# Attention and feed-forward on one core: the second batch's q and k turned on TensorE, the first batch reordered

## The chip, the cores and the metric

The kernel runs on one core of a Trainium2 chip. The metric is the device time of one execution in microseconds, shown as the median of the runs.

## The reference

For 8 batches the reference computes grouped-query attention, with 16 query heads over 4 key/value heads, 384 tokens and head width 64, and then a feed-forward layer whose activation is a squared ReLU:

```python
k, v = repeat(k, 4), repeat(v, 4)                   # 4 -> 16 heads
attn = softmax(q @ k.T / 8)                         # per head, 384 x 384
x    = (attn @ v) -> [3072 tokens, 1024]
h    = max(x @ w_in, 0)                             # 1024 -> 2048
out  = (h * h) @ w_out                              # 2048 -> 1024
```

Inputs and output are float32; the kernel multiplies in bfloat16.

## The kernel before, in words

The work is cut into 64 pairs of heads, eight to a batch (`NPB`); pair p belongs to batch p // 8. A pair needs kT (the keys of its key/value head, turned so that the head width lies on the partitions, and doubled, so that both heads of a pair have a copy) and qT (its queries, turned alike). TensorE forms the scores of a pair into PSUM, ScalarE takes their exponential (`expT`), TensorE multiplies it with the values, which carry a column of ones, into `po` (`attend`, L382), and VectorE divides by the column sums (L389, L392) into `o_sb`. The result is turned once more into `xT`, the feed-forward's input. A batch's feed-forward has 128 up matmuls (16 tiles of 8, L408) and 96 down matmuls (6 tiles of 16, L426). Each up tile is clipped on VectorE and squared on ScalarE into `h2T`; each down tile is copied to `y_sb` and stored from SP's queue.

A `Recorder` (L8) takes every operation in program order, with the tiles that it reads and writes, and adds the semaphore waits. Each engine issues its own operations strictly in recorded order, so whatever is recorded behind a waiting operation on the same engine waits too.

**First batch.** Its q, k and v come by plain loads; GpSimd casts q chunk by chunk (`cast_q`, L228) and between the casts issues the loads of `w_in` in eight parts. kT, qT and xT are turned on TensorE by `turn_on_pe` (L268): three 128x128 transposing matmuls against an identity into a PSUM bank, and a VectorE copy out (L278). Scores come in three units a pair (`scores_unit`, L332, two matmuls at L339), each with its own exponential (L345) and two sets of PSUM banks in turn. Matmuls on a zeroed tile (`idle`, L252) fill the gaps.

**Later batches.** `prepare(b)` (L298) doubles k on VectorE (L301), then issues three DMA transposes from SP's queue: kT (L304), and qT in two halves (L311, pairs 0 to 3 and 4 to 7 of the batch), and then the loads of k and q for batch b + 2 from GpSimd's queue. `prepare_v` does the values. For batch 1, `prepare(1)` is called inside the first feed-forward; for the others, in the fifth pair of the batch before (`n % NPB == 4`). Scores of a pair come in one go (`scores_pair`, L348, matmuls at L355) with one exponential (L372). `put_x` (L395) turns `o_sb` into `xT` by a DMA transpose on SP's queue.

**Order.** `feed_forward` is a generator of steps of four matmuls. `fill(ns)` records as many steps as a budget buys, at 165 ns an up matmul and 216 ns a down matmul; `ready` holds the last batch whose feed-forward may run. After the first batch, `fill(8000)`, `prepare(1)`, `prepare_v(1)` and `fill(12000)` come before pair 8. Then each pair records its scores, a fill of 0.4, the values of the head before, a fill of 0.2, the other head, `put_x`, and a fill of 0.4 of `PER_PAIR`, which is 2600 in batch 1 (pairs 8 to 15) and 5000 after it. While pairs 8 to 15 run, only the first feed-forward may be drawn from, so it has to last for them; the second one may begin with pair 17.

Of the kernel before, what the change touches and what calls it, by code (L numbers as in the profile page):

```python
# [5 lines left out]
ALU = mybir.AluOpType  # L6
# [100 lines left out]
def bass_gqa_attention__then__ffn_squared_relu_kernel(  # L107
# [12 lines left out]
    HKV = 4  # L120
# [37 lines left out]
    po = nc.alloc_psum_tensor("po", [128, 512], f32)  # L158
    f_ps = [nc.alloc_psum_tensor(f"f_ps{i}", [128, 512], f32) for i in range(2)]
    po_v = po[:, 0:NJ * 2 * (D + 1)].rearrange("p (i s e) -> p i s e", i=NJ, s=2)  # L160
    sc_flat = sc_ps.ap().rearrange("p b c -> p (b c)")


# [64 lines left out]
    def cast_q(c):  # L228
        R.add("gpsimd", lambda g: g.tensor_copy(q_st[0][:, 2 * c:2 * c + 2, :], q_f[:, 2 * c:2 * c + 2, :]),  # L229
              reads=[("q_f", c)], writes=[("q_st", 0, c)])  # L230

    cast_q(0)
    cast_q(1)
    R.add("gpsimd", lambda g: g.tensor_copy(
        v_aug[0][:, :, 0:D], v_f.ap().rearrange("p g j d -> p (g j) d")),
        reads=["v_f"], writes=[("v_aug", 0)])
    load_w_in(0)
    for c in range(2, NPB):
        cast_q(c)
        load_w_in(c - 1)  # L240
# [11 lines left out]
    def idle(count):  # L252
# [4 lines left out]

        R.add("tensor", mm, reads=["warm"], writes=[("f_ps", 1)])


    banks = [0]

    def turn_bank():
        i = banks[0] % 2
        banks[0] += 1
        return [(sc_ps[:, 4].bitcast(bf16), ("sc", 4)), (f_ps[0].ap().bitcast(bf16), ("f_ps", 0))][i]

    def turn_on_pe(src, src_keys, dst, dst_key):  # L268
        ps, key = turn_bank()

        def tr(pe):
            for t in range(NJ):
                m = pe.matmul(ps[:, t * 128:(t + 1) * 128], src[:, t * 128:(t + 1) * 128], ident[:],  # L273
                              is_transpose=True)
            return m

        R.add("tensor", tr, reads=[*src_keys, "ident"], writes=[key])
        R.add("vector", lambda e: e.tensor_copy(dst, ps[:, 0:S]), reads=[key], writes=[dst_key])  # L278

    def dup_k(b, g):  # L280
        src = (k_f if b == 0 else k_st[b % NKS])[:, g].unsqueeze(2).to_broadcast([128, NJ, 2, D])
        R.add("vector", lambda e: e.tensor_copy(k_dup[b % 2][:, g * NJ:(g + 1) * NJ], src),
              reads=[("k_f", g) if b == 0 else ("k_st", b % NKS)], writes=[("k_dup", b % 2, g)])

    def first_kT(g):
        dup_k(0, g)
        turn_on_pe(k_dup[0][:, g * NJ:(g + 1) * NJ].rearrange("p a x d -> p (a x d)"), [("k_dup", 0, g)],
                   kT[0][:, g], ("kT", 0, g))

    def first_qT(c):  # L290
        turn_on_pe(q_st[0][:, 2 * c:2 * c + 2, :].rearrange("p h e -> p (h e)"), [("q_st", 0, c)],
                   qT[0][:, c], ("qT", 0, c))

    def first_oT(c):
        turn_on_pe(o_sb[c % NO].ap().rearrange("p i s d -> p (i s d)"), [("o_sb", c % NO)],
                   xT[0][:, c], ("xT", 0, c))

    def prepare(b):  # L298
        st = b % NST
        src = k_st[b % NKS].ap().rearrange("p g j d -> p (g j) d").unsqueeze(2)  # L300
        R.add("vector", lambda e: e.tensor_copy(  # L301
            k_dup[b % 2][:, :, :, :], src.to_broadcast([128, HKV * NJ, 2, D])),
            reads=[("k_st", b % NKS)], writes=[("k_dup", b % 2, g) for g in range(HKV)])
        R.add("sync", lambda e: e.dma_start_transpose(  # L304
            kT[b % 2].ap().rearrange("p g (j c) -> p (g j) c", j=NJ),
            k_dup[b % 2].ap().rearrange("p a x d -> p (a x d)")),
            reads=[("k_dup", b % 2, g) for g in range(HKV)],
            writes=[("kT", b % 2, g) for g in range(HKV)], dma=f"kt{b % 2}")
        for part in range(2):
            cs = range(4 * part, 4 * part + 4)  # L310
            R.add("sync", lambda e, cs=cs: e.dma_start_transpose(  # L311
                qT[b % 2][:, cs.start:cs.stop, :].rearrange("p h (t c) -> p (h t) c", t=NJ),
                q_st[st][:, 2 * cs.start:2 * cs.stop, :].rearrange("p h e -> p (h e)")),
                reads=[("q_st", st, c) for c in cs], writes=[("qT", b % 2, c) for c in cs],
                dma=f"qt{b % 2}_{part}")
        if b + 2 < B and b >= 1:
            load_k(b + 2)
            if b > 1:
                load_q(b + 2)

    def prepare_v(b):
        R.add("vector", lambda e: e.tensor_copy(
# [49 lines left out]
        R.add("scalar", lambda e: e.activation(dst, src, AF.Exp, scale=0.125),  # L372
              reads=sc_keys, writes=[("expT", p % NEX, j) for j in range(NJ)])

    def attend(p, s):
        b, g = p // NPB, (p % NPB) // 2

        def av(pe):
            for i in range(NJ):
                f = NJ * s + i  # L380
                for j in range(NJ):
                    m = pe.matmul(po_v[:, i, s, :], expT[p % NEX][:, j, f * 128:(f + 1) * 128],  # L382
                                  v_aug[b % 2][:, g * NJ + j, :], start=(j == 0), stop=(j == NJ - 1))
            return m

        R.add("tensor", av, reads=[("expT", p % NEX, j) for j in range(NJ)] +
              [("v_aug", b % 2), ("v_one", b % 2)], writes=["po"])
        if s == 1:
            R.add("vector", lambda e: e.reciprocal(rinv[p % 2].ap().unsqueeze(3), po_v[:, :, :, D:D + 1]),  # L389
                  reads=["po"], writes=[("rinv", p % 2)])  # L390
            rb = rinv[p % 2].ap().unsqueeze(3).to_broadcast([128, NJ, 2, D])
            R.add("vector", lambda e: e.tensor_tensor(o_sb[p % NO][:, :, :, :], po_v[:, :, :, 0:D], rb, ALU.mult),  # L392
                  reads=["po", ("rinv", p % 2)], writes=[("o_sb", p % NO)])

    def put_x(p):  # L395
        b, c = p // NPB, p % NPB
        R.add("sync", lambda e: e.dma_start_transpose(
            xT[b % NXT][:, c, :].rearrange("p (i c) -> p i c", i=NJ),
            o_sb[p % NO].ap().rearrange("p i s d -> p (i s d)")),
            reads=[("o_sb", p % NO)], writes=[("xT", b % NXT, c)], dma=f"xt{p % 8}")  # L400


    tiles = [0]

    def up_step(b, c, half, u, r):
        def mm(pe):
            for kc in range(4 * half, 4 * half + 4):
                m = pe.matmul(f_ps[u][:, 0:S], w_in_sb[:, kc, c * 128:(c + 1) * 128],  # L408
                              xT[b % NXT][:, kc, :], start=(kc == 0), stop=(kc == NKC - 1))
            return m  # L410

        R.add("tensor", mm, reads=[("w_in", c * 128 // WC)] +
              [("xT", b % NXT, kc) for kc in range(4 * half, 4 * half + 4)], writes=[("f_ps", u)])
        if half == 1:
            R.add("vector", lambda e: e.tensor_scalar_max(hr[r][:, :], f_ps[u][:, 0:S], 0.0),  # L415
                  reads=[("f_ps", u)], writes=[("hr", r)])
            R.add("scalar", lambda e: e.activation(h2T[b % 2][:, c, :], hr[r][:, :], AF.Square),  # L417
                  reads=[("hr", r)], writes=[("h2T", b % 2, c)])
        return 4 * 165

    def down_step(b, i, jj, part, u):
        yb = (b * 2 * NJ + jj * NJ + i) % NY
# [17 lines left out]
        return 4 * 216  # L440

    def feed_forward(b):
        for c in range(NFC):
            for half in range(2):
                yield up_step(b, c, half, tiles[0] % 2, tiles[0] % NHR)
            tiles[0] += 1
        for jj in range(2):
            for i in range(NJ):
                for part in range(4):
                    yield down_step(b, i, jj, part, tiles[0] % 2)  # L450
                tiles[0] += 1


    ready = [-1]

    def all_feed_forward():
        for b in range(B):
# [3 lines left out]

    ffn = all_feed_forward()
    credit = [0.0]
    FIRST, SECOND = 8000.0, 12000.0
    PER_PAIR = {1: 2600.0, **{b: 5000.0 for b in range(2, B + 1)}}

    def fill(ns):
        credit[0] += ns
# [4 lines left out]
                return  # L473
            credit[0] -= t

    idle(12)
    first_kT(0)
    first_qT(0)
    first_qT(1)
    for n in range(NPB):  # L480
        scores_unit(n, 0)
        if n + 2 < NPB:
            if n % 2 == 0:
                first_kT((n + 2) // 2)
            first_qT(n + 2)
        else:
            idle(1)
        scores_unit(n, 1)
        idle(1)
        if n >= 1:  # L490
            attend(n - 1, 0)
        scores_unit(n, 2)
        idle(1)
        if n >= 1:
            attend(n - 1, 1)
        if n >= 2:
            first_oT(n - 2)
    idle(2)
    attend(NPB - 1, 0)
    first_oT(NPB - 2)  # L500
    attend(NPB - 1, 1)
    idle(5)
    first_oT(NPB - 1)
    load_q(3)
    ready[0] = 0
    fill(FIRST)
    prepare(1)
    prepare_v(1)
    fill(SECOND)
    for n in range(NPB, NP + 1):  # L510
        per = PER_PAIR[n // NPB]
        if n < NP:
            scores_pair(n)
        fill(per * 0.4)
        if n > NPB:
            attend(n - 1, 0)
        fill(per * 0.2)
        if n > NPB:
            attend(n - 1, 1)
            put_x(n - 1)  # L520
        if n % NPB == 4 and n // NPB + 1 < B:
            prepare(n // NPB + 1)
        if n % NPB == 7 and n // NPB + 1 < B:
            prepare_v(n // NPB + 1)
        fill(per * 0.4)
        ready[0] = max(0, n // NPB - 1)
# [32 lines left out]
```

## Time and profile before

| | us |
|---|---|
| median of 3 runs (464.14 to 468.75) | 466.71 |
| the profiled execution | 464.65 |
| its span, first to last instruction | 462.9 |

The span is what the trace's times count from; some 1.75 us of the profiled execution lie around it. PE is TensorE's matmul row, DVE is VectorE, ACT is ScalarE, POOL is GpSimd, SP the engine whose queue carries stores and DMA transposes. A busy share is an average over stages; which wait ends last in a stage is read from the chain of waits and from the timeline.

### The profile page before, as it was taken

Reading aid. Unit: us, or ns where it says so; the run is one execution under the profiler, and the core shown is the slowest. Engines: PE = TensorE matmul, PEld = TensorE weight load, DVE = VectorE, ACT = ScalarE, POOL = GpSimd, SP = SyncE. Lnnn points to the kernel's source line nnn. Section 1 sums busy time; section 2 is a strip of 40 time slices with the busy share of each in tenths; the row PEclk is TensorE's granted clock in tenths of the full one; section 3 lists DMA queues with packets and bytes.
Section 4 is the critical chain, followed back from the end, with each engine's and each line's share of the span. In section 5 each row is a group of like instructions: output and inputs, shape, how many; then the busy total and the mean of one; then the engine's idle time right before and its main releaser. Section 6 shows DMA issues by size and latency. Waiting matters only on the chain.

```text
span 462.9 us, 8137 instructions
## 1 busy us (share of the span) xinstructions
PE 433.8 (94%) x3557; PEld 241.0 (52%) x3593; DVE 162.9 (35%) x343; ACT 199.2 (43%) x209; POOL 33.3 (7%) x48
## 2 busy tenths in 40 slices
PE   7889729968999999999999999999999999999997
PEld 3455415535654466555654566555654566545543
DVE  2454302323432344323443344223443244323411
ACT  3673315534663355434663266434562366302300
POOL 6921000200020001000020000000000000000000
PEclk9999959988999999999999999999999999999999
DMA  9999999592049411982099115221152210121012
GB/s 236 197 196 204 194 181 176 115 185 77 13 55 176 139 41 20 169 152 64 18 121 186 64 33 101 62 86 62 28 111 64 76 41 19 41 84 39 0 59 79
DMA packets 100643, 45.88 MB, mean 99 GB/s; under 512 B 79104, under 2 KB 94464, under 8 KB 100608
## 3 DMA queue, kind: packets, MB, share of 16 engines
q0 software_dynamic: 34288, 16.65, 28.6%
q1 hardware_dynamic: 64208, 27.15, 25.1%
q10 hardware_dynamic: 2112, 1.57, 1.1%
q8 instruction: 28, 0.46, 0.4%
q14 instruction: 7, 0.06, 0.0%
HBM read 35.65 MB, written 12.58 MB: 104 GB/s over the span
## 4 chain that ended last, share of the span: by engine, by line
PE 90%; DMA 5%; DVE 2%; issue 2%; POOL 1%; SPq 0%; ACTq 0%
PE f_ps L426 36%; PE f_ps L408 35%; PE po L382 8%; PE sc_ps L355 7%; DMA qT<-q_st 4%; PE sc_ps L339 1%; PE f_ps L255 1%; DMA q_f<-in_q_dram 1%; DVE o_sb L392 1%; DMA xT<-o_sb 1%; PE sc_ps L273 0%; PE f_ps L273 0%; DVE hr L415 0%; POOL q_st L229 0%; DVE xT L278 0%
## 5 line engine op out<-in xcount | busy, mean ns | idle before, releaser
L408 PE MATMUL f_ps<-xT,w_in_sb 128*128 128x384 bf16 x1024 | 181.2, 327 | 2.3 <-DMA xT<-o_sb 1.9
L426 PE MATMUL f_ps<-w_out_sb,h2T 128*128 128x512 bf16 x732 | 177.9, 382 | 2.3 <-issue 0.5
L372 ACT ACTIVATE expT<-sc_ps 128x2304 bf16<-128x2304 f32 x56 | 116.8, 2086 | 111.7 <-PE sc_ps L355 110.4
L408 PEld LDWEIGHTS f_ps<-xT,w_in_sb 128*128 128x128 bf16 x1024 | 94.5, 98 | 65.7 <-issue 6.8
L417 ACT ACTIVATE h2T<-hr 128x384 bf16<-128x384 f32 x128 | 66.7, 521 | 117.1 <-DVE hr L415 115.9
L415 DVE TENSOR_SCALAR hr<-f_ps 128x384 f32<-128x384 f32 x128 | 71.3, 557 | 116.8 <-PE f_ps L408 116.8
L426 PEld LDWEIGHTS f_ps<-w_out_sb,h2T 128*128 128x128 bf16 x768 | 69.0, 98 | 76.9 <-issue 8.4
L435 DVE COPY y_sb<-f_ps 128x512 f32<-128x512 f32 x48 | 33.2, 692 | 114.0 <-PE f_ps L426 113.5
L382 PEld LDWEIGHTS po<-v_aug,expT 128*128 128x128 bf16 x1152 | 54.5, 99 | 22.3 <-DVE o_sb L392 0.8
L382 PE MATMUL po<-v_aug,expT 128*128 128x65 bf16 x1152 | 58.5, 196 | 0.6 <-DVE o_sb L392 0.5
L355 PE MATMUL sc_ps<-qT,kT 64*128 64x128 bf16 (+2 forms) x504 | 38.6, 279 | 14.9 <-DMA qT<-q_st 11.0
L355 PEld LDWEIGHTS sc_ps<-qT,kT 64*128 64x128 bf16 x504 | 21.3, 96 | 36.6 <-issue 20.9
L392 DVE TENSOR_TENSOR o_sb<-po,rinv 128x384 bf16<-128x384 f32 x64 | 35.7, 557 | 2.2
L389 DVE RECIPROCAL rinv<-po 128x6 f32<-128x6 f32 x64 | 12.3, 192 | 54.1 <-PE po L382 54.1
L345 ACT ACTIVATE expT<-sc_ps 128x768 bf16<-128x768 f32 x24 | 18.4, 811 | 9.3 <-PE sc_ps L339 9.1
L166 POOL DMA_DIRECT2D k_st<-in_k_dram x7 | 5.3, 760 | 196.8 <-DVE k_dup L301 179.7
L255 PE MATMUL f_ps<-warm 128*128 128x256 bf16 x37 | 9.6, 343 | 1.1 <-DVE warm L220 1.1
L339 PE MATMUL sc_ps<-qT,kT 64*128 64x384 bf16 x48 | 9.6, 397 | 0.0
L180 POOL DMA_DIRECT2D q_st<-in_q_dram x7 | 8.2, 1173 | 1.5 <-PE sc_ps L339 1.5
L188 POOL DMA_DIRECT2D w_in_sb<-in_moe_w_in_dram x8 | 7.2, 896 | 0.0
L255 PEld LDWEIGHTS f_ps<-warm 128*128 128x128 bf16 x37 | 4.0, 113 | 5.7 <-issue 4.0
L173 POOL DMA_DIRECT2D v_st<-in_v_dram x7 | 5.5, 780 | 0.0
(34 smaller groups left out, 40.3 us busy)
## 6 DMA issues: line engine op xcount, KB each, us to landing
out_dram<-y_sb SPq DMA_DIRECT2D x48, 256.0 KB, 2.0
q_st<-in_q_dram POOLq DMA_DIRECT2D x7, 768.0 KB, 12.7
w_in_sb<-in_moe_w_in_dram POOLq DMA_DIRECT2D x8, 512.0 KB, 11.5
w_out_sb<-in_moe_w_out_dram POOLq DMA_DIRECT2D x2, 2048.0 KB, 36.0
k_st<-in_k_dram POOLq DMA_DIRECT2D x7, 192.0 KB, 4.1
v_st<-in_v_dram POOLq DMA_DIRECT2D x7, 192.0 KB, 14.2
xT<-o_sb SPq DMA_TRANSPOSE x56, 2.4
q_f<-in_q_dram ACTq DMA_DIRECT2D x1, 768.0 KB, 7.8
```

Of the source, the lines that this page charges most:

```text
L255: m = pe.matmul(f_ps[1][:, 0:256], warm[:, 0:128], warm[:, 0:256])
L339: m = pe.matmul(sc_ps[:, 2 * u + x, 0:S], kt[rows, j * 128:(j + 1) * 128], qt[rows, :])
L345: R.add("scalar", lambda e: e.activation(dst, src, AF.Exp, scale=0.125), reads=[("sc", 2 * u), ("sc", 2 * u + 1)], writes=[("expT", p % NE ...
L355: return pe.matmul(sc_flat[:, at + c0:at + c1], kt[rows, j * 128:(j + 1) * 128], qt[rows, c0:c1])
L372: R.add("scalar", lambda e: e.activation(dst, src, AF.Exp, scale=0.125), reads=sc_keys, writes=[("expT", p % NEX, j) for j in range(NJ)])
L382: m = pe.matmul(po_v[:, i, s, :], expT[p % NEX][:, j, f * 128:(f + 1) * 128], v_aug[b % 2][:, g * NJ + j, :], start=(j == 0), stop=(j == N ...
L392: R.add("vector", lambda e: e.tensor_tensor(o_sb[p % NO][:, :, :, :], po_v[:, :, :, 0:D], rb, ALU.mult), reads=["po", ("rinv", p % 2)], wr ...
L408: m = pe.matmul(f_ps[u][:, 0:S], w_in_sb[:, kc, c * 128:(c + 1) * 128], xT[b % NXT][:, kc, :], start=(kc == 0), stop=(kc == NKC - 1))
L415: R.add("vector", lambda e: e.tensor_scalar_max(hr[r][:, :], f_ps[u][:, 0:S], 0.0), reads=[("f_ps", u)], writes=[("hr", r)])
L417: R.add("scalar", lambda e: e.activation(h2T[b % 2][:, c, :], hr[r][:, :], AF.Square), reads=[("hr", r)], writes=[("h2T", b % 2, c)])
L426: m = pe.matmul(f_ps[u][:, :], h2T[b % 2][:, c, i * 128:(i + 1) * 128], w_out_sb[:, c, jj * 512:(jj + 1) * 512], start=(c == 0), stop=(c = ...
L435: R.add("vector", lambda e: e.tensor_copy(y_sb[yb][:, :], f_ps[u][:, :]), reads=[("f_ps", u)], writes=[("y", yb)])
```

## The change

On TensorE, kT and qT of batch 1 are turned by the first batch's functions, spread over the fills of the first feed-forward, into sc_ps banks 0 to 3; the three DMA transposes of batch 1 fall away. The fills before pair 8 become 6000, 1500, four of 700 and eight of 500; `PER_PAIR` of batch 1 becomes 3200. `prepare(2)` is called in pair 14 instead of pair 12; the later ones stay where they were. In the first batch, kT and qT are turned one pair ahead, behind the second score unit, most `idle` matmuls are placed anew, six two-chunk steps of the first two up tiles are recorded in pairs 5 and 6 and behind pair 7, and the last pair's two heads are normalised separately. The first load of `w_in` is issued ahead of the second cast of q. The diff, cut to its core:

```diff
 # setup
+    po_alt = sc_ps[:, 1, 0:NJ * 2 * (D + 1)].rearrange("p (i s e) -> p i s e", i=NJ, s=2)
...
     cast_q(0)
+    load_w_in(0)
     cast_q(1)
...                                            # (cast of v stands here)
-    load_w_in(0)
     for c in range(2, NPB):
...
+    def idle_on_sc(count):                      # idle() into sc_ps bank 3
...
-    banks = [0]
-    def turn_bank():
-        i = banks[0] % 2
-        banks[0] += 1
-        return [(sc_ps[:, 4].bitcast(bf16), ("sc", 4)), (f_ps[0].ap().bitcast(bf16), ("f_ps", 0))][i]
-    def turn_on_pe(src, src_keys, dst, dst_key):
-        ps, key = turn_bank()
+    slots = [0]
+    RING, FREE = (4, 5), (0, 1, 2, 3)           # 0 to 4: sc_ps banks; 5: f_ps[1]
+    def turn_bank(banks):
+        i = banks[slots[0] % len(banks)]
+        slots[0] += 1
+        if i == 5:
+            return f_ps[1].ap().bitcast(bf16)[:, 0:S], ("f_ps", 1)
+        return sc_bf[:, i, 0:S], ("sc", i)
+    def turn_on_pe(src, src_keys, dst, dst_key, banks):
+        ps, key = turn_bank(banks)
...
-    def first_kT(g):
-        dup_k(0, g)
-        turn_on_pe(k_dup[0][...], [("k_dup", 0, g)], kT[0][:, g], ("kT", 0, g))
+    def first_kT(g, b=0):
+        if b == 0:
+            dup_k(0, g)
+        turn_on_pe(k_dup[b][...], [("k_dup", b, g)], kT[b][:, g], ("kT", b, g), FREE if b else RING)
+    def first_qT(c, b=0): ...                   # likewise, with q_st[b], qT[b]
+    def first_oT(c, banks=RING): ...
+    def dup_all_k(b):                           # first half of the old prepare()
...
+        if b + 2 < B:
+            load_k(b + 2)
     def prepare(b):
+        dup_all_k(b)
...                                            # the DMA transposes of kT and qT
-        if b + 2 < B and b >= 1:
-            load_k(b + 2)
-            if b > 1:
-                load_q(b + 2)
+        if b + 2 < B:
+            load_q(b + 2)
...
-    def attend(p, s):
+    def attend(p, s, alone=False):              # alone: each head by itself, the
...                                            # second in po_alt (sc_ps bank 1)
-    def up_step(b, c, half, u, r):
+    def up_step(b, c, k0, k1, u, r):            # chunks k0 to k1 instead of a half
...
     def feed_forward(b):
-        for c in range(NFC):
-            for half in range(2):
-                yield up_step(b, c, half, tiles[0] % 2, tiles[0] % NHR)
+        first = 0
+        if b == 0:
+            for c, k in ((0, 0), (0, 2), (0, 4), (1, 0), (1, 2), (1, 4), (0, 6), (1, 6)):
+                yield up_step(b, c, k, k + 2, c, c)
+            tiles[0] += 2
+            first = 2
+        for c in range(first, NFC):
+            for k in range(0, NKC, 4):
+                yield up_step(b, c, k, k + 4, tiles[0] % 2, tiles[0] % NHR)
             tiles[0] += 1
...
-    ready = [-1]
+    ready = [0]
...
-    FIRST, SECOND = 8000.0, 12000.0
-    PER_PAIR = {1: 2600.0, **{b: 5000.0 for b in range(2, B + 1)}}
+    PER_PAIR = {1: 3200.0, **{b: 5000.0 for b in range(2, B + 1)}}
...
-    idle(12)
+    idle(13)
     first_kT(0)
+    idle(2)
     first_qT(0)
-    first_qT(1)
+    idle(3)
     for n in range(NPB):
+        early = n in (5, 6)
         scores_unit(n, 0)
-        if n + 2 < NPB:
-            if n % 2 == 0:
-                first_kT((n + 2) // 2)
-            first_qT(n + 2)
-        else:
-            idle(1)
-        scores_unit(n, 1)
-        idle(1)
+        if early:
+            next(ffn)
+        elif n < 2:
+            idle(2 - n)
         if n >= 1:
             attend(n - 1, 0)
+        scores_unit(n, 1)
+        if n % 2 == 1 and n + 1 < NPB:
+            first_kT((n + 1) // 2)
+        if n + 1 < NPB:
+            first_qT(n + 1)
+        if n >= 1:
+            attend(n - 1, 1)
         scores_unit(n, 2)
         idle(1)
-        if n >= 1:
-            attend(n - 1, 1)
         if n >= 2:
             first_oT(n - 2)
-    idle(2)
-    attend(NPB - 1, 0)
-    first_oT(NPB - 2)
-    attend(NPB - 1, 1)
-    idle(5)
-    first_oT(NPB - 1)
+    next(ffn)
+    attend(NPB - 1, 0, True)
+    first_oT(NPB - 2, (4,))
+    attend(NPB - 1, 1, True)
+    for _ in range(3):
+        next(ffn)
+    idle_on_sc(2)
+    first_oT(NPB - 1, (0,))
+    idle_on_sc(3)
     load_q(3)
-    ready[0] = 0
-    fill(FIRST)
-    prepare(1)
+    fill(6000.0)
+    dup_all_k(1)
+    fill(1500.0)
+    for g in range(HKV):
+        first_kT(g, 1)
+        fill(700.0)
     prepare_v(1)
-    fill(SECOND)
+    for c in range(NPB):
+        first_qT(c, 1)
+        fill(500.0)
     for n in range(NPB, NP + 1):
...
-        if n % NPB == 4 and n // NPB + 1 < B:
+        if n % NPB == (6 if n < 2 * NPB else 4) and n // NPB + 1 < B:
             prepare(n // NPB + 1)

```

## Rows read from the trace of the kernel before

**Rows 1.** The page: busy time and, in 40 slices of 11.6 us, granted clock and DMA share.
```profile
PE 433.8 (94%) x3557; PEld 241.0 (52%) x3593; DVE 162.9 (35%) x343; ACT 199.2 (43%) x209; POOL 33.3 (7%) x48
...
PEclk9999959988999999999999999999999999999999
DMA  9999999592049411982099115221152210121012
```

**Rows 2.** Waits of PE, longest first: total us, times, longest us.
```profile
PE sc_ps L355 <- DMA qT<-q_st: 11.0, 1, 11.0
PE sc_ps L355 <- issue: 3.8, 1, 3.8
```

**Rows 3.** Chain that ended last, 34 to 112 us: start, us, what.
```profile
34.83 11.89 PE f_ps L408 x72
...
47.97 18.13 DMA qT<-q_st
...
75.10 0.59 PE sc_ps L355 x8
...
82.82 0.59 PE sc_ps L355 x8
...
98.25 3.79 issue
102.04 1.11 PE sc_ps L355 x8
...
107.67 2.34 DMA xT<-o_sb
110.05 2.12 PE f_ps L408 x12
```

**Rows 4.** The same chain in the first batch, 11 to 25 us.
```profile
11.45 0.43 PE sc_ps L339 x2
...
12.21 0.50 PE po L382 x9
...
15.81 0.32 PE f_ps L273 x3
...
24.74 0.17 PE f_ps L273 x3
```

**Rows 5.** Timeline, 0 to 32 us: start, busy us, instruction, idle before it and releaser.
```profile
4.47 0.50 PE L273 MATMUL f_ps<-ident,q_st 128*128 128x128 bf16 x3
5.01 0.36 DVE L278 COPY qT<-f_ps 128x384 bf16<-128x384 bf16 x1 [0.16 <-PE f_ps L273]
...
6.81 0.50 PE L339 MATMUL sc_ps<-qT,kT 64*128 64x384 bf16 x2
...
7.35 0.81 ACT L345 ACTIVATE expT<-sc_ps 128x768 bf16<-128x768 f32 x1 [3.24 <-PE sc_ps L339]
...
15.31 0.50 PE L273 MATMUL sc_ps<-ident,k_dup 128*128 128x128 bf16 x3 [0.91 <-DVE k_dup L282]
...
18.89 0.39 PE L339 MATMUL sc_ps<-qT,kT 64*128 64x384 bf16 x2
...
23.51 8.35 ACT L345 ACTIVATE expT<-sc_ps 128x768 bf16<-128x768 f32 x11 [1.14 <-PE sc_ps L339]
```

**Rows 6.** Instructions on qT, batches 2 and 6: duration ns, first and last start; landing.
```profile
L311 SPq DMA_TRANSPOSE qT<-q_st x1: 5562/5562/5562, 90.1 to 90.1; - x1
DMA to landing us min/median/max: 11.8/11.8/11.8
...
L311 SPq DMA_TRANSPOSE qT<-q_st x1: 1790/1790/1790, 285.1 to 285.1; - x1
DMA to landing us min/median/max: 4.2/4.2/4.2
```

**Rows 7.** Loads of q for batches 1 and 2, issued at 17.5 and 22.4: us to landing.
```profile
q_st<-in_q_dram POOLq DMA_DIRECT2D x1, 768.0 KB, 20.1
...
q_st<-in_q_dram POOLq DMA_DIRECT2D x1, 768.0 KB, 49.4
```

More of the change, by code (lines that the diff above doesn't have):

```diff
@@ L258, in idle, with mm @@
         R.add("tensor", mm, reads=["warm"], writes=[("f_ps", 1)])
-    banks = [0]
-    def turn_bank():
-        i = banks[0] % 2
-        banks[0] += 1
-        return [(sc_ps[:, 4].bitcast(bf16), ("sc", 4)), (f_ps[0].ap().bitcast(bf16), ("f_ps", 0))][i]
-    def turn_on_pe(src, src_keys, dst, dst_key):
-        ps, key = turn_bank()
+    def idle_on_sc(count):
+        def mm(pe):
+            for _ in range(count):
+                m = pe.matmul(sc_ps[:, 3, 0:256], warm[:, 0:128], warm[:, 0:256])
+            return m
+        R.add("tensor", mm, reads=["warm"], writes=[("sc", 3)])
+    slots = [0]
+    RING, FREE = (4, 5), (0, 1, 2, 3)
+    sc_bf = sc_ps.ap().bitcast(bf16)
+    def turn_bank(banks):
[6 more added lines that the diff above has]
+        ps, key = turn_bank(banks)
         def tr(pe):
@@ L277, in turn_on_pe @@
         R.add("tensor", tr, reads=[*src_keys, "ident"], writes=[key])
-        R.add("vector", lambda e: e.tensor_copy(dst, ps[:, 0:S]), reads=[key], writes=[dst_key])
+        R.add("vector", lambda e: e.tensor_copy(dst, ps), reads=[key], writes=[dst_key])
     def dup_k(b, g):
@@ L283, in dup_k, with first_qT, first_oT @@
               reads=[("k_f", g) if b == 0 else ("k_st", b % NKS)], writes=[("k_dup", b % 2, g)])
-    def first_kT(g):
-        dup_k(0, g)
[L287 to L299, printed above, removed]
+    def first_kT(g, b=0):
+        if b == 0:
+            dup_k(0, g)
+        turn_on_pe(k_dup[b][:, g * NJ:(g + 1) * NJ].rearrange("p a x d -> p (a x d)"), [("k_dup", b, g)],
+                   kT[b][:, g], ("kT", b, g), FREE if b else RING)
+    def first_qT(c, b=0):
+        turn_on_pe(q_st[b][:, 2 * c:2 * c + 2, :].rearrange("p h e -> p (h e)"), [("q_st", b, c)],
+                   qT[b][:, c], ("qT", b, c), FREE if b else RING)
+    def first_oT(c, banks=RING):
+        turn_on_pe(o_sb[c % NO].ap().rearrange("p i s d -> p (i s d)"), [("o_sb", c % NO, x) for x in range(2)],
+                   xT[0][:, c], ("xT", 0, c), banks)
+    def dup_all_k(b):
         src = k_st[b % NKS].ap().rearrange("p g j d -> p (g j) d").unsqueeze(2)
@@ L303, in prepare @@
             reads=[("k_st", b % NKS)], writes=[("k_dup", b % 2, g) for g in range(HKV)])
+        if b + 2 < B:
+            load_k(b + 2)
+    def prepare(b):
+        st = b % NST
+        dup_all_k(b)
         R.add("sync", lambda e: e.dma_start_transpose(
@@ L373, in scores_pair @@
               reads=sc_keys, writes=[("expT", p % NEX, j) for j in range(NJ)])
-    def attend(p, s):
+    def attend(p, s, alone=False):
         b, g = p // NPB, (p % NPB) // 2
+        acc, acc_key = (po_alt, ("sc", 1)) if alone and s == 1 else (po_v, "po")
         def av(pe):
@@ L381, in av @@
                 for j in range(NJ):
-                    m = pe.matmul(po_v[:, i, s, :], expT[p % NEX][:, j, f * 128:(f + 1) * 128],
+                    m = pe.matmul(acc[:, i, s, :], expT[p % NEX][:, j, f * 128:(f + 1) * 128],
                                   v_aug[b % 2][:, g * NJ + j, :], start=(j == 0), stop=(j == NJ - 1))
@@ L386, in attend @@
         R.add("tensor", av, reads=[("expT", p % NEX, j) for j in range(NJ)] +
[L387 to L393, printed above, removed]
+              [("v_aug", b % 2), ("v_one", b % 2)], writes=[acc_key])
+        if alone or s == 1:
+            ss = slice(s, s + 1) if alone else slice(0, 2)
+            w = ss.stop - ss.start
+            rinv_v = rinv[p % 2][:, :, ss].unsqueeze(3)
+            R.add("vector", lambda e: e.reciprocal(rinv_v, acc[:, :, ss, D:D + 1]),
+                  reads=[acc_key], writes=[("rinv", p % 2)])
+            rb = rinv_v.to_broadcast([128, NJ, w, D])
+            R.add("vector", lambda e: e.tensor_tensor(o_sb[p % NO][:, :, ss, :], acc[:, :, ss, 0:D], rb, ALU.mult),
+                  reads=[acc_key, ("rinv", p % 2)], writes=[("o_sb", p % NO, s)])
     def put_x(p):
@@ L399, in put_x @@
             o_sb[p % NO].ap().rearrange("p i s d -> p (i s d)")),
-            reads=[("o_sb", p % NO)], writes=[("xT", b % NXT, c)], dma=f"xt{p % 8}")
+            reads=[("o_sb", p % NO, x) for x in range(2)], writes=[("xT", b % NXT, c)], dma=f"xt{p % 8}")
     tiles = [0]
-    def up_step(b, c, half, u, r):
+    def up_step(b, c, k0, k1, u, r):
         def mm(pe):
-            for kc in range(4 * half, 4 * half + 4):
+            for kc in range(k0, k1):
                 m = pe.matmul(f_ps[u][:, 0:S], w_in_sb[:, kc, c * 128:(c + 1) * 128],
@@ L412, in up_step @@
         R.add("tensor", mm, reads=[("w_in", c * 128 // WC)] +
-              [("xT", b % NXT, kc) for kc in range(4 * half, 4 * half + 4)], writes=[("f_ps", u)])
-        if half == 1:
+              [("xT", b % NXT, kc) for kc in range(k0, k1)], writes=[("f_ps", u)])
+        if k1 == NKC:
             R.add("vector", lambda e: e.tensor_scalar_max(hr[r][:, :], f_ps[u][:, 0:S], 0.0),
@@ L418, in up_step @@
                   reads=[("hr", r)], writes=[("h2T", b % 2, c)])
-        return 4 * 165
+        return (k1 - k0) * 165
     def down_step(b, i, jj, part, u):
```

## The prediction

> **What bounds the kernel now.** I read the page first. TensorE is busy 94% of the span, and the slices place the rest: the granted clock dips only around 70 us and 100 us, and the DMA engines are full for the first seven slices, that is to 81 us [rows 1]. A kernel so full of matmuls gains only where TensorE waits, so the waits of PE come next. Two matter, both of scores at L355: 11.0 us for a DMA transpose of q, and 3.8 us put down to "issue" [rows 2]. The chain of waits tells what they are. The first up matmuls run from 34.83 us; the transpose of qT issued at 47.97 us takes 18.13 us to land, and pair 8 starts behind it. The "issue" ends at 102.04 us, with pair 16, the first of batch 2 [rows 3]. Its qT half was issued at 90.1 us and landed 11.8 us later, at 101.9 us [rows 6], so this too is a DMA transpose. Before 34.83 us lies the first batch, bound by a chain of small steps, and there the same work has two prices: a turn of three transposes takes 0.32 us of the chain at 15.81 us and 0.17 us at 24.74 us [rows 4]. That is TensorE's lower level (1.2 GHz) and then its upper one (2.4 GHz); the matmuls at 18.89 us are the first shorter ones, and what went before is 3.6 us without an idle row from 15.31 us on [rows 5]. (The page's clock line does not show this stretch as low; the durations do.)
>
> From pair 16 on nothing in the change alters the work, so its worth is how much earlier pair 16 and what follows it run.
>
> **First batch.** Before, the first exponential starts at 7.35 us, as scores at 6.81 us stood behind the turn of the second q chunk [rows 5]. Now they stand behind the first chunk's turn. This turn ends near 5.0 us, its copy takes 0.36 us [rows 5], and idle(3) writes the bank that the copy reads, so it waits for it; with three idle matmuls of 0.21 us scores start near 6.1 us. The load of w_in ahead of the second cast I cost at nothing: the cast waits for its q anyway, so the gap covers the issue. A pair at the lower level is bound by TensorE: 3 score units of 0.43, 2 halves of values of 0.50, 2.5 turns of 0.32 [rows 4] and some 0.3 for an idle matmul make 3.4 us. A pair at the upper level is bound by ScalarE: the last eleven exponentials take 8.35 us, 0.76 each [rows 5], 2.28 us a pair. When the clock rises I take from the trace, near 18.9 us; before it, pair 0 (without values) takes 2.3 us and pairs 1 to 3 some 3.45 us each, to 18.7 us, and four pairs of 2.28 us end the exponentials at 28.0 us. Before they end at 31.9 us (23.51 + 8.35). Bounds: never rising gives 33 us, rising with pair 1 gives 25 us.
>
> Behind the last exponential the kernel now takes 3.0 us to the first up matmul (31.9 to 34.8). The new tail has the same links, values, normalising, turn, copy; normalising is in halves, so I take 2.7 us. The steady feed-forward starts at 30.7 us, with twelve up matmuls already done: they cover the wait of that tail and ScalarE's time in pairs 5 and 6.
>
> **The turn of batch 1.** Removed: three DMA transposes and the 11.0 us wait. Added on TensorE: 4 + 8 turns of 0.17 us, 2.0 us; on VectorE 12 copies of 0.36 us, 4.3 us, hidden because an up tile costs TensorE 1.32 us (8 x 11.89/72) and VectorE some 0.6 us. The turns wait for the load of q, which lands at 17.5 + 20.1 = 37.6 us [rows 7]; the first q turn comes at 30.7 + 7.5 + 0.7 + 2.8 = 41.7 us, so it does not wait, but the margin is 4 us and everything of TensorE is queued behind it. The fills before pair 8 come to 14.3 us at 165 ns, which is also what the trace has (11.89/72, rows 3). Pair 8 starts at 30.7 + 14.3 + 2.0 = 47.0 us instead of 66.15.
>
> Here the Trainium skill speaks against the change. What the rows show is 0.17 us for three transposes in the middle of other matmuls [rows 4], 56 ns each. "TensorE: Matmul & The Clock Gate", Part 4 (PE-mode transpose), gives about 275 ns for a transpose in a kernel and says that the upper clock level doesn't engage for it; by that the 36 transposes would cost 9.9 us and the sum would be 462. The trace disagrees, as its transposes ran at the upper level, but among matmuls that hold it there.
>
> **Pairs 8 to 15.** A pair takes 3.86 us now ((82.82 - 75.10)/2, rows 3), of which 2.60 is the fill. With 3.2 us of fill it takes 4.46 us. The budgets still spend the whole first feed-forward: 6 early steps of 330 ns, 14.3 us and 25.6 us make 41.88 us against its 41.86. So pair 16 is reached at 47.0 + 8 x 4.46 = 82.7 us, 15.5 us earlier than 98.25, and the four down matmuls now left over for it are gone.
>
> **The new wait.** prepare(2) moves from pair 12 to pair 14. Before, the qT half is issued 7.3 us after its pair starts (82.82 to 90.1) and lands 11.8 us later [rows 3, 6]. Pair 14 starts at 47.0 + 6 x 4.46 = 73.8 us; its larger fill puts the call 0.4 us later; so qT lands at 73.8 + 0.4 + 7.3 + 11.8 = 93.3 us. Pair 16 would wait 10.6 us instead of 3.8. Queued behind this wait on TensorE are the values of pair 15, and with them xT and the second feed-forward, since the first is used up. The 11.8 us are the term that decides most. The same transpose took 4.2 us in batch 6, where no load of later q and k runs beside it [rows 6], and 18.1 us for batch 1 under the full load of weights [rows 3]. I take 11.8, because prepare(2) still starts the loads of batch 4 beside the transposes; the ends stay for the range. Batch 2's q itself is there: 22.4 + 49.4 = 71.8 us [rows 7], and earlier without batch 1's transposes beside it; were it late, SP's stores and xT turns would be queued behind it.
>
> **Behind pair 16.** The up matmuls now flow from 110.05 us, 8.0 us after pair 16's scores; the values of pair 15 stood behind four leftover down matmuls (1.9 us on the chain at the lower level), and SP's queue had stores and turns to work off before the last xT, 2.34 us [rows 3]. Now: scores 1.1, exponential 2.1, scores of pair 17 1.1, four up matmuls 1.3, some 5.7 us. That is worth 2.3 us, at least nothing.
>
> **Sum.** 102.04 - 93.3 = 8.7 earlier at pair 16, 2.3 behind it: 11.0 us off the profiled execution's 464.65 gives 453.7. The median of the runs is 2.1 us above that execution, the lowest run 0.5 below; I set the forecast at 455 as a median, about half of that difference added.
>
> **Rivals.**
> - *The transpose is quick.* If batch 4's loads delay it little, qT lands by row 6's 4.2 us at 85.7 us, and the wait at pair 16 shrinks to 3 us. Then 455 - 7.6 = 447. For: the other loads are over by then. Against: all of batches 2 to 5 start loads in the same call, and batch 2 shows 11.8. 0.22.
> - *The first batch stays at 1.2 GHz.* There are fewer idle matmuls in a pair than now (one instead of two or three). Exponentials end at 33, the tail and the first fills cost 1 to 2 us more, and all behind shifts by 6.5: 461. Against: there are no idle rows in the new order, and the rise came after such a stretch. 0.13.
> - *A late landing.* Transposes of batch 2 meet what is left of the loads and take the 18.1 us of batch 1: 461. 0.06. If q of batch 1 lands 5 to 10 us later than now, TensorE stands there as long, the forecast moves as much, to 460 to 465, and the old wait has only changed its place. 0.04.
> - *Turns break the stream.* If a turn costs the 0.5 us that its record alone covers at 4.47 us [rows 5], not 0.17, twelve cost 4 us more: 459. The Trainium skill's page named above would make it 7.9 us more. 0.04.
> - *Slower: the clock does not rise with the feed-forward either,* since its first stage now has transposes in it. The lower level costs 1 us for each 1 us of matmul work at the upper one. The late first batch uses up 6.5 of the 11 us; from 4.5 us of such work at the start of the feed-forward on it is a loss, from 9.5 us on one of over 1%, and if all 16 us up to pair 8 run low, the time is 455 + 6.5 + 16 = 477. Against: the chain at the 72 up matmuls is at the upper level throughout. 0.05.
> - The change not doing what it says is hardly open: the transposes of batch 1 fall away in the code.
>
> **How the numbers follow.** The forecast keeps 0.46; its own range is 450 to 459. Below it the quick transpose reaches 447, and an early rise of the clock (25 us instead of 28) takes another 3. Above lie the cases to 461, and the runs' own spread of 2 us. The range is 444 to 463. About 1% is what a measurement of this kernel tells from no change: 462 and 471. Faster takes the forecast, the quick transpose and most of the low-clock, late and turn cases: 0.84. Within 1%: 0.11. Slower: 0.05.
>
> **What would show it.** Pair 8 near 47 us, with no idle row of PE before it; twelve copies in the up stage and the three transposing matmuls at 0.17 us of the chain; the first short matmuls before 19 us; the exponentials' end near 28 us; pair 16 reached near 83 us and waiting some 10 us for a qT issued near 81.5 us; equal durations per line from then on. Wrong it would be if qT for pair 16 lands before TensorE asks (more gained), if TensorE waits for q of batch 1 inside the feed-forward, or if matmuls of the first batch keep their long durations to its end.

## The result and the profile after

The changed kernel takes 454.59 us (median of 4 runs, 453.37 to 454.97), the kernel before 467.22 us (median of 4): a ratio of 0.9733, 95% interval 0.9679 to 0.9788. Every ratio here leaves out runs more than 1.5% above the fastest run of the same kernel, which concerns two runs of one experiment. The profiled spans are 462.9 and 453.2 us, 9.7 us apart; the medians lie 12.6 us apart because the profiled execution of before (464.65 us) was 2.6 us under its own median and that of after (454.95 us) 0.4 us above.

The page after, first part and slices (of 11.3 us each), against [rows 1]:

```profile
PE 430.9 (95%) x3591; PEld 241.1 (53%) x3626; DVE 165.7 (37%) x357; ACT 198.8 (44%) x209; POOL 33.2 (7%) x48
...
PEclk9999999759999999999999999999999999999999
DMA  9999999960099207921296206121432210220011
```

The clock's dip of slice 6 (58 to 69 us) is gone; one dip is left, in slices 8 and 9, from 79 to 102 us. The longest waits of PE after:

```profile
PE sc_ps L372 <- DMA qT<-q_st: 11.3, 1, 11.3
PE sc_ps L372 <- ACT expT L389: 1.1, 1, 1.1
```

There is one wait for a DMA transpose where there were two [rows 2], and it is as long as the longer of these. The chain shows that it is the other one. After, 29 to 106 us:

```profile
29.90 0.51 PE f_ps L429 x2
30.41 0.02 issue
30.44 0.57 DVE hr L436
31.01 0.05 issue
31.05 7.32 PE f_ps L429 x44
38.38 0.17 PE sc_ps L286 x3
38.55 0.65 PE f_ps L429 x4
...
45.94 0.37 DVE hr L436
46.31 0.10 issue
46.42 0.62 DVE qT L291 x2
47.04 0.05 issue
47.09 0.66 PE sc_ps L372 x8
...
73.42 0.59 PE sc_ps L372 x8
...
80.05 13.20 DMA qT<-q_st
93.25 0.09 issue
93.34 1.17 PE sc_ps L372 x9
...
97.82 4.62 PE f_ps L429 x16
...
105.60 0.59 PE sc_ps L372 x8
```

L286 is `turn_on_pe` now, L429 an up matmul, L372 the scores of a pair. Pair 8 starts at 47.09 us instead of 66.15 us, 19.1 us earlier. Pair 16 starts at 93.34 us instead of 102.04 us, only 8.7 us earlier. Of the difference, 2.9 us are feed-forward work, which the larger fills moved in front of pair 16; the other 7.5 us are lost to the longer wait (11.3 us instead of 3.8) for the qT of batch 2, whose first half is issued at 80.05 us and takes 13.2 us to land [rows 3 and 6 for before]. Pair 18, at 105.60 us, stood here in the kernel before:

```profile
115.34 0.59 PE sc_ps L355 x8
```

That is 9.74 us, and the same difference is left at the end of the span. So nothing is won or lost behind pair 18.

The first batch after, on the timeline of PE and ACT:

```profile
5.71 0.67 PE L256 MATMUL f_ps<-warm 128*128 128x256 bf16 x3 [0.45 <-DVE qT L291]
6.31 0.34 PE L356 MATMUL sc_ps<-qT,kT 64*128 64x384 bf16 x2
...
9.79 0.33 PE L286 MATMUL sc_ps<-ident,q_st 128*128 128x128 bf16 x3
...
22.90 3.97 ACT L362 ACTIVATE expT<-sc_ps 128x768 bf16<-128x768 f32 x5 [0.48 <-PE sc_ps L356]
```

The first scores already have the short duration, 0.34 us against 0.50 [rows 5], so TensorE is at 2.4 GHz from 6.3 us on and not from 18.9 us. The last exponential ends at 26.87 us (22.90 + 3.97) instead of 31.86.

### The profile page after: what moved, and what is told of

It reads as the page before. It is cut to its first block, busy times and chain, and to the rows that moved or that the text cites. A ratio compares the mean times of both kernels' runs of the same rounds, so it can differ in the third digit from the quotient of the medians.

```text
span 453.2 us, 8216 instructions
## 1 busy us (share of the span) xinstructions
PE 430.9 (95%) x3591; PEld 241.1 (53%) x3626; DVE 165.7 (37%) x357; ACT 198.8 (44%) x209; POOL 33.2 (7%) x48
## 4 chain that ended last, share of the span: by engine, by line
PE 91%; DMA 3%; DVE 2%; ACT 2%; issue 1%; SPq 0%
PE f_ps L429 38%; PE f_ps L447 36%; PE po L400 8%; PE sc_ps L372 7%; DMA qT<-q_st 3%; ACT expT L362 1%; PE f_ps L256 1%; PE sc_ps L286 1%; PE sc_ps L356 1%; ACT expT L389 0%; DVE o_sb L413 0%; DVE qT L291 0%; SPq L323 0%; DVE hr L436 0%; DVE y_sb L456 0%
## 5 line engine op out<-in xcount | busy, mean ns | idle before, releaser
L429 PE MATMUL f_ps<-xT,w_in_sb 128*128 128x384 bf16 x1024 | 184.6, 329 | 1.2 <-DVE xT L291 0.7
L447 PE MATMUL f_ps<-w_out_sb,h2T 128*128 128x512 bf16 x733 | 176.0, 379 | 2.0 <-issue 0.2
L429 PEld LDWEIGHTS f_ps<-xT,w_in_sb 128*128 128x128 bf16 x1024 | 94.1, 98 | 64.2 <-issue 8.0
L400 PEld LDWEIGHTS po<-v_aug,expT 128*128 128x128 bf16 x1143 | 52.1, 98 | 23.8 <-ACT expT L362 2.6
L400 PE MATMUL po<-v_aug,expT 128*128 128x65 bf16 x1143 | 56.9, 194 | 1.3 <-ACT expT L362 0.9
L372 PE MATMUL sc_ps<-qT,kT 64*128 64x128 bf16 (+2 forms) x504 | 38.1, 276 | 12.8 <-DMA qT<-q_st 11.3
L372 PEld LDWEIGHTS sc_ps<-qT,kT 64*128 64x128 bf16 x504 | 21.1, 95 | 34.4 <-issue 28.0
L362 ACT ACTIVATE expT<-sc_ps 128x768 bf16<-128x768 f32 x24 | 18.4, 810 | 4.4 <-PE sc_ps L356 3.6
L256 PE MATMUL f_ps<-warm 128*128 128x256 bf16 x29 | 7.2, 360 | 1.5 <-DVE warm L221 1.1
L356 PE MATMUL sc_ps<-qT,kT 64*128 64x384 bf16 x48 | 8.1, 332 | 0.3 <-ACT expT L362 0.2
```

Source lines behind the costliest of these rows:

```text
L256: m = pe.matmul(f_ps[1][:, 0:256], warm[:, 0:128], warm[:, 0:256])
L356: m = pe.matmul(sc_ps[:, 2 * u + x, 0:S], kt[rows, j * 128:(j + 1) * 128], qt[rows, :])
L372: return pe.matmul(sc_flat[:, at + c0:at + c1], kt[rows, j * 128:(j + 1) * 128], qt[rows, c0:c1])
L400: m = pe.matmul(acc[:, i, s, :], expT[p % NEX][:, j, f * 128:(f + 1) * 128], v_aug[b % 2][:, g * NJ + j, :], start=(j == 0), stop=(j == NJ ...
L447: m = pe.matmul(f_ps[u][:, :], h2T[b % 2][:, c, i * 128:(i + 1) * 128], w_out_sb[:, c, jj * 512:(jj + 1) * 512], start=(c == 0), stop=(c = ...
```

## Experiments

The theory after the result: the change removed the wait at pair 8 and shortened the first batch; about 7.5 us of this were lost again at pair 16, because prepare(2) is called two pairs later and because the loads of batch 4, started by the same call, slow the transposes. The rivals: the place of the call does not matter; the transposes are slow by themselves; a wait removed at one pair is only moved to the next. Ratios are to the kernel before; the changed kernel has 0.9733. The kernel before was run again beside the experiments, with medians of 465.4 and 465.7 us instead of 467.2, so times of different experiments compare to some 2 us only, and ratios and traces go before them.

**prepare(2) in pair 12 again.**

```diff
-        if n % NPB == (6 if n < 2 * NPB else 4) and n // NPB + 1 < B:
+        if n % NPB == 4 and n // NPB + 1 < B:
```

> prepare(2) is called in pair 12 again, everything else as in the changed kernel. Theory (the wait of 11.3 us at pair 16 stands because the call comes two pairs later): the qT half is issued near 71.5 us (pair 12 at 64.8 us, plus 6.6) instead of 80.05; beside it run the last loads of batch 3 and those of batch 4, so it takes 13 to 18 us and lands at 84.5 to 89.5 us; TensorE, there at 82 us, waits 2.5 to 7.5 us; 447 to 451 us. Rival (the place of the call does not matter, the transposes end when the loads do): pair 16 again near 93 us, 454 to 455 us.

450.61 us, ratio 0.9668 (0.9630 to 0.9707). The chain there:

```profile
73.95 14.77 DMA qT<-q_st
88.81 1.17 PE sc_ps L372 x9
```

and its longest wait of PE:

```profile
PE sc_ps L372 <- DMA qT<-q_st: 7.2, 1, 7.2
```

The half is issued 6.1 us earlier than in the changed kernel and lands 4.5 us earlier, as it takes 1.6 us longer, and the wait is 7.2 us instead of 11.3. It is issued 2.4 us later than expected, as kT held SP's queue for 3.75 us instead of 1.52. Pair 18 starts at 101.00 us, 4.6 us earlier than in the changed kernel; the medians lie 4.0 us apart, while the two ratios' intervals overlap. So by the traces the move to pair 14 was a loss of some 4 us inside a change that gained.

**The loads of batch 4 behind pair 16, prepare(2) in pair 14.**

```diff
     # dup_all_k, prepare, prepare_v: no load_k, load_q, load_v where b == 2
+        if n == 2 * NPB:                 # right behind scores_pair(16)
+            at = [len(R.ops) - 1]        # its exponential
+            load_k(4, at); load_q(4, at); load_v(4, at)
```

> prepare(2) stays in pair 14, but the loads of k, q and v of batch 4 wait for pair 16's exponential. Theory (the loads beside the DMA transposes make them slow): the qT half issued near 80 us lands in 4 to 6 us instead of 13.2, pair 16 starts at 84 to 86 us instead of 93.3; 445 to 448 us. Rival (the transpose queue is slow by itself): it still takes 11 us or more; 453 to 455 us.

447.84 us, ratio 0.9614 (0.9573 to 0.9655). The chain, and below it the instructions on kT in that stretch, of this kernel and then of the changed one:

```profile
80.15 4.35 DMA qT<-q_st
...
84.59 0.65 PE sc_ps L372 x8
...
87.43 4.23 DMA xT<-o_sb
91.71 4.02 PE f_ps L429 x12
```

```profile
L323 SPq DMA_TRANSPOSE kT<-k_dup x1: 1512/1512/1512, 78.6 to 78.6; - x1
DMA to landing us min/median/max: 4.6/4.6/4.6
```

```profile
L323 SPq DMA_TRANSPOSE kT<-k_dup x1: 1516/1516/1516, 78.5 to 78.5; - x1
DMA to landing us min/median/max: 8.4/8.4/8.4
```

The calls stand at the same times; only the loads beside them are gone, and qT lands in 4.35 us instead of 13.2, kT in 4.6 instead of 8.4. The rival of a slow queue is out. Not all of it is kept: pair 16 starts 8.75 us earlier than in the changed kernel, pair 18 only 5.8 us (99.79 us). The loads now start at 87.70 us, beside the xT of pair 15, which takes 4.23 us instead of 2.34 [rows 3], and the twelve up matmuls behind it run at the lower level, 0.335 us each.

**Both.** The last two edits together.

> prepare(2) in pair 12 and the loads of batch 4 behind pair 16's exponential. Theory: the qT half is issued near 71.5 us and lands before 82 us, so TensorE does not wait at pair 16 and its clock does not fall there: 11.3 us and 1 to 2 us more off, 441 to 443 us. Rival (another wait stands right behind that one, for xT of pair 15 or for the late loads of batch 4 at prepare(4)): 445 us or more.

Its four runs took 441.93, 446.68, 449.64 and 450.08 us, farther apart than those of any other experiment; the ratio, 0.9533 (0.9450 to 0.9616), goes by the two lower ones. The trace is of the slowest run. The chain:

```profile
81.89 0.60 PE sc_ps L372 x8
...
85.75 7.57 DMA xT<-o_sb
```

Pair 16 no longer waits for qT. But the loads now start with its exponential, beside the transpose that turns pair 15's result into xT, and this took 7.57 us where it took 2.34 [rows 3]. So in this execution the rival came true: the wait stands one transpose further on, and it is loads again that run beside it, as with the 4.23 us of the experiment before. Whether the two quicker runs had this wait is not known: one has a time that the theory gave, the other one that the rival gave.

**The same, with the loads behind that xT.**

```diff
+        if n == 2 * NPB:                 # right behind put_x(15)
+            at = [len(R.ops) - 1]        # its DMA transpose
+            load_k(4, at); load_q(4, at); load_v(4, at)
```

> prepare(2) in pair 12, and the loads of batch 4 wait until the turn of pair 15's result into xT has landed. Theory (in the kernel with prepare(2) in pair 12 and loads behind pair 16's exponential, the wait of 7.3 us for this xT came from those loads beside it): xT lands in 2 to 3 us instead of 7.6, the wait shrinks to about 2 us, the clock stays up, 441 to 443 us. Rival (the DMA transpose of xT is slow for another reason, such as the queue behind stores): 446 us or more.

444.91 us, ratio 0.9547 (0.9508 to 0.9586). The chain:

```profile
85.48 2.31 DMA xT<-o_sb
87.83 4.02 PE f_ps L429 x12
```

xT lands in 2.31 us and the wait for it is 2.3 us, as expected. That this is worth time can't be told from the runs, as the ratio's interval overlaps with that of the last experiment. The time is 2 us over the expectation: the twelve up matmuls behind the wait took 0.335 us each instead of 0.165, so the clock was at its lower level after all, with TensorE idle for 1.5 and 2.3 us in the 6 us before.

**The same, with 2600 a pair in batch 1.**

```diff
-    PER_PAIR = {1: 3200.0, **{b: 5000.0 for b in range(2, B + 1)}}
+    PER_PAIR = {1: 2600.0, **{b: 5000.0 for b in range(2, B + 1)}}
```

> As the kernel whose loads of batch 4 wait for xT of pair 15, and in addition the fill of a pair in batch 1 is 2600 instead of 3200, so that 4.8 us of the first feed-forward are left for pair 16. Theory (what is left of the wait behind pair 16 is TensorE without work, and leftover steps cover it): another 1 to 2 us less than that kernel, 439 to 442 us. Rival (pair 16 is reached 4.8 us earlier, near 77 us, before its qT, which lands near 78 us, and the wait only changes its place): the same time as that kernel.

443.76 us, ratio 0.9521 (0.9481 to 0.9562), the lowest ratio here and clear of the changed kernel's. The chain:

```profile
70.42 9.15 DMA qT<-q_st
79.65 0.97 PE sc_ps L372 x8
```

Both theory and rival have part: the leftover steps cover the wait for xT, and pair 16, reached 4 us earlier, waits 2.3 us for qT instead. This half took 9.15 us although the loads of batch 4 had not begun; for its first 3.9 us the load of batch 3's q, issued at 24.8 us, still ran beside it, to 74.3 us. What else slowed it is not shown. The interval overlaps with that of the kernel with 3200 (444.91 us), so whether the share of a pair is worth anything stays open.

**Batch 1 by DMA transposes again.**

```diff
-    dup_all_k(1)
-    fill(1500.0)
-    for g in range(HKV):
-        first_kT(g, 1)
-        fill(700.0)
-    prepare_v(1)
-    for c in range(NPB):
-        first_qT(c, 1)
-        fill(500.0)
+    prepare(1)                           # without load_q(3), issued before
+    prepare_v(1)
+    fill(8300.0)
```

> kT and qT of batch 1 go by the three DMA transposes again, called where the changed kernel doubles k; the first batch's new order, the fills' sum and all that follows stay. Theory (the turn on TensorE is worth the wait of pair 8): qT is issued near 41 us under the loads of the weights and lands near 59 us, TensorE runs dry near 44 us and pair 8 starts at 59 to 60 us instead of 47.1; with the same wait at pair 16 the time is 465 to 467 us. Rival (part of this wait would only be moved from pair 8 to pair 16 and is not lost twice): pair 16 starts no more than 6 us later, 458 to 461 us.

472.39 us, ratio 1.0127 (1.0076 to 1.0178): 1.3% slower than before the change. Waits and chain:

```profile
PE sc_ps L372 <- DMA qT<-q_st: 28.1, 2, 16.6
```

```profile
41.71 21.18 DMA qT<-q_st
62.94 1.14 PE sc_ps L372 x8
69.14 0.59 PE sc_ps L372 x8
```

Both waits stand, 28.1 us together; none was taken in by the other, because prepare(2) hangs on pair 14 and moves with it. The expectation was 5 us short: qT landed at 62.9 us instead of 59, and pair 8, at the lower clock behind the wait, took 6.2 us instead of 4.0.

**The first batch in its old order.** The edit puts the old loop, its idle matmuls and its two turning banks (sc_ps 4 and f_ps 0) back, without early steps:

```diff
-    idle(13)
+    idle(12)
     first_kT(0)
-    idle(2)
     first_qT(0)
-    idle(3)
+    first_qT(1)
...
-    fill(6000.0)
+    fill(7980.0)
```

> The first batch in its old order, with its old idle matmuls, without the six early steps (their budget goes to the first fill) and with the load of w_in at its old place; the turn of batch 1 and all that follows as in the changed kernel. Theory (the first batch's order brings what the flow of up matmuls gains, and nothing behind takes it back, because prepare(2) hangs on pair 14): up matmuls from 34.8 us, pair 8 at 52 to 53 us instead of 47.1, all of it 5 to 6 us later, 459 to 461 us. Rival (the wait at pair 16 takes the difference in): 454 to 456 us.

461.01 us, ratio 0.9889 (0.9848 to 0.9929): as expected, 6.4 us over the changed kernel, with pair 8 at 54.07 us, 1 us later than expected. Which part of the new order brings how much (the turns one pair ahead, the early steps, the two heads apart, the load of w_in) no run tells. Its first matmuls tell something of the clock (line numbers are shifted by two: L288 is a turn, L358 scores, L402 values):

```profile
6.31 0.33 PE L288 MATMUL sc_ps<-ident,q_st 128*128 128x128 bf16 x3 [1.42 <-POOL q_st L230]
6.57 0.34 PE L358 MATMUL sc_ps<-qT,kT 64*128 64x384 bf16 x2
8.31 0.34 PE L288 MATMUL f_ps<-ident,k_dup 128*128 128x128 bf16 x3 [1.40 <-DVE k_dup L297]
8.89 0.50 PE L288 MATMUL sc_ps<-ident,q_st 128*128 128x128 bf16 x3 [0.24 <-POOL q_st L230]
...
18.26 0.70 PE L402 MATMUL po<-v_aug,expT 128*128 128x65 bf16 x9
18.78 0.35 PE L288 MATMUL sc_ps<-ident,o_sb 128*128 128x128 bf16 x3
```

Here too TensorE stood at 2.4 GHz from 6.3 us, but after waits of 1.42 and 1.40 us it was back at 1.2 GHz at 8.9 us and stayed there until 18.8 us. The kernel before, which issues the same first instructions, had no such early rise in its trace: its scores at 6.81 us took 0.50 us [rows 5].

**The early idle matmuls left out.**

```diff
-    idle(13)
+    idle(12)
     first_kT(0)
-    idle(2)
     first_qT(0)
-    idle(3)
```

> At the very start 12 idle matmuls instead of 13, and the two and three idle matmuls around the first turn of q left out. Theory (these matmuls are what lets the clock rise at 6.3 us): the first scores come 0.6 us earlier, but matmuls of the first batch keep the long durations of the lower level until pair 1 or later, up to 18.9 us as in the kernel before; the last exponential ends 1 to 3 us later than 26.9 us, and the time is 455.5 to 458 us. Rival (the rise does not hang on them): the first batch ends 0.5 us earlier, 454 us or a little less.

455.01 us, ratio 0.9754 (0.9718 to 0.9790). On the timeline the first batch did what the theory said:

```profile
12.36 0.67 PE L400 MATMUL po<-v_aug,expT 128*128 128x65 bf16 x9
12.97 0.44 PE L356 MATMUL sc_ps<-qT,kT 64*128 64x384 bf16 x2
13.34 0.34 PE L286 MATMUL f_ps<-ident,q_st 128*128 128x128 bf16 x3
```

The lower level lasts to 13 us, the last exponential ends at 27.97 us instead of 26.87, and pair 8 starts at 48.18 us instead of 47.09. But pair 16 starts only 0.4 us later, as its qT landed in 12.5 us instead of 13.2, and the time is under the expected range. So these six idle matmuls are worth 1.1 us in the first batch and nothing that this measurement can tell at the end. That they alone let the clock rise at 6.3 us is not shown: the kernel with the old order has no idle matmuls there either, and its trace does rise at 6.3 us. There is one trace of each kernel.

## Why the prediction was right

The forecast was 455 us, the median is 454.59; the sum was 11.0 us, the profiles differ by 9.7. That the forecast is 0.4 us from the median is luck: the sum gave 453.7 us for the profiled execution, which took 454.95, and the 1.3 us added for the median make up for that. Term by term:

| step (us) | predicted | measured |
|---|---|---|
| clock rises in the first batch | 18.9 | 6.3 |
| last exponential ends | 28.0 | 26.87 |
| up matmuls flow from | 30.7 | 29.90 |
| from there to pair 8 | 16.3 | 17.19 |
| pair 8 starts | 47.0 | 47.09 |
| one pair of batch 1 | 4.46 | 4.39 |
| pair 14 starts | 73.8 | 73.42 |
| its start to the issue of qT | 7.7 | 6.63 |
| issue to landing | 11.8 | 13.20 |
| pair 16 starts | 93.3 | 93.34 |
| gain behind pair 16 | 2.3 | 1.04 |

The mechanism held in the main: the wait at pair 8 gone, turns in the up stage at 0.17 us, and a longer wait at pair 16 from a call two pairs later. Undoing the parts one at a time shows that each counts: without batch 1's turn the kernel is 17.8 us slower (472.39 - 454.59), without the first batch's new order 6.4 us, and with the call in pair 12 it is 4.0 us faster. These don't add up to the gain of 12.6 us, because the parts meet at the same waits: with the DMA transposes of batch 1, the earlier first batch only waits longer at pair 8 (16.6 us instead of 11.0). That pair 16 came out to 0.04 us is partly luck, as errors of the table's steps cancel (-0.8, +0.9, -0.5, -1.1 and +1.4 us). The errors:

- *When the clock rises I take from the trace, near 18.9 us* was wrong. TensorE was at 2.4 GHz from 6.3 us and stayed there to pair 16's wait; the experiment with the old order lost the level again by 8.9 us, after two waits that the new order does not have. That an early rise would end the exponentials at 25 us was wrong too: they end at 26.87, at 2.5 us a pair (20.2 us for 8) instead of 2.28. ScalarE was busy for 18.4 of these 20.2 us, close to the 18.2 predicted, and stood still for 1.8 us between exponentials. In pairs 3 and 5 the chain runs through VectorE's copies and normalising, from 15.1 and 20.1 us; how much of the 1.8 us comes from there is not shown.
- *Hidden because an up tile costs TensorE 1.32 us*: true of ten copies of twelve. The last clip and the last two qT copies stand on the chain from 45.9 to 47.1 us, which costs TensorE some 0.35 us (its last four up matmuls start at 46.08 us and last 0.65), and about 0.5 us more are lost at 30.4 us, where both early tiles end together and TensorE waits for their clip. The two make up the 0.9 us by which this stage came out longer.
- The landing of qT was 1.4 us under and its issue 1.1 us over the measured. That the transposes meet loads was the reason given for 11.8 rather than 4.2 us; the kernel without these loads shows 4.35.
- *Behind pair 16* was mis-sized by 1.3 us. I counted four up matmuls at the lower level; sixteen ran there, in 4.62 us (0.29 each) instead of 2.6. Before, the stall for xT stood where these slow matmuls stand now.

Of the rivals, the quick transpose is what would have happened without batch 4's loads (447.84 measured there against 447 worked out, though pair 16 came earlier than worked out and part of this was lost behind it). The low clock in the first batch did not come, turns did not break the stream, and no load was late: q of batch 1 landed at 37.1 us, before its first turn at 41.49 us, and batch 2's qT took 13.2 us and not 18.1. Against the about 0.275 us for one transpose in a kernel of the Trainium skill's "TensorE: Matmul & The Clock Gate", Part 4 (PE-mode transpose), stand 0.17 us for three (38.38 us in the chain), at the upper level. The record of one lasts 0.22 us there (0.31 us at the lower level, at 4.0 us); three cost the chain less than one record, as neighbours' records overlap. Slower was out: the clock stayed up until pair 16's wait.

## What to carry to other kernels

A wait removed early in a chain is worth only what the next fixed event lets through: look for the next transfer that is issued from a later place, and move its issue as far as the wait moved. Before pricing a DMA transpose, look at what the same call starts beside it; keep bulk loads behind the transposes that TensorE is about to wait for, and then check the next transpose behind them too.

## What the runs showed of the hardware

A DMA transpose of half of a batch's q took 13.2 us beside the loads of one batch's q, k and v (1.15 MB), and 4.35 us without them, at the same time of the kernel; one of xT took 4.23 us beside such loads and 2.31 us ahead of them. TensorE's higher level was lost within 2.6 us of the first short matmul, with waits of 1.42 us just before it and 1.40 us inside (old first order), and in the 6 us with idle rows of 1.5 and 2.3 us before 87.8 us (loads behind xT); with 2600 a pair it was lost at a single wait of 2.33 us, behind which pair 16's scores took 0.97 us on the chain instead of 0.59. The profile's granted clock is no safe guide to the first 19 us: it reads 1.00 there in the kernel before, whose scores take 0.50 us, and from 9 to 19 us 0.51 with the old first order and 1.00 with the new one, as the durations do. So the durations of equal matmuls are the surer reading.
